# Zero matmuls during the first loads and two weight pieces ahead of the loop, in a windowed attention with a three-way max layer

## The chip, the cores and the metric

The kernel runs on one core of one Trainium2 chip. The core has a matrix engine (PE, TensorE), a vector engine (DVE), a scalar engine (ACT), a general engine (POOL, GpSimd) and a queue processor (SP, SyncE) that issues most transfers; sixteen DMA engines carry them. The metric is device time in microseconds of one execution; the median of some executions is compared.

## The reference

Eight batches of eight heads attend over 512 local and 32 global tokens of width 64. A local query sees the 32 global keys and the local keys at most 32 positions away; a global query sees all keys. The output of each token (8 heads by 64 = 512 numbers) goes through a layer with three weight matrices, an elementwise maximum, and an output matrix:

```python
k_all = np.concatenate([k_g, k_l], axis=2)
s_g = scale * np.matmul(q_g, k_all.transpose(0, 1, 3, 2))
out_g = np.matmul(sm(s_g), v_all)
mask = np.abs(pos[:, None] - pos[None, :]) <= window
s_ll = np.where(mask, s_ll, -1000000000.0)
a_l = sm(np.concatenate([s_lg, s_ll], axis=-1))
out_l = np.matmul(a_l, np.concatenate([v_g, v_l], axis=2))
...
h = np.maximum(np.maximum(x @ w1, x @ w2), x @ w3)
return (h @ w_out).astype(np.float32)
```

There are 4352 tokens (8 times 544). The maximum layer goes from 512 to 768 and back to 512. The weights arrive as 64-bit floats.

## The kernel before

**Attention.** Work is cut into 128 tiles `sl`: pair of heads `p = sl // 4`, and a quarter `t` of 128 queries. A tile passes these steps, each with an engine's line: `load_q` (L250) brings the queries, `scores` multiplies them with the window's keys on PE (L335 for the first 28 tiles, which are kept in f32) into a bank `S`, DVE adds the mask and scales and keeps the row extreme (L342), ACT takes the exponential and its sum (L344), DVE takes the reciprocal (L347, L348) and one of DVE, ACT and POOL multiplies (L121, L123, L125). `trans` turns the result on PE into a bank `T` (L362, L363), a copy takes it out as `pt`, and `pv` multiplies it with the values on PE (L401) into a bank `O`, copied to `xr`. `split_x` (L424, L425) makes a high and a low part of `xr`, the tile `xs`, which feeds the maximum layer. The first sixteen tiles go through the two halves of the queries in the order `SEQ`, with half key blocks from `load_half` (L216); their softmax lies in a constant tile `early`.

**Weights.** There are 24 pieces of 128 by 512 numbers: 18 of the three matrices and 6 of the output matrix. `load_weight` (L165) brings the 64-bit piece, 512 KB, into `raw`. `convert` makes two f32 parts of it on the chip, in three steps: ACT takes the absolute value of the high words (L175) and DVE does two scalar passes (L176, L177); DVE joins sign and low bits in two passes (L180, L181); a cast (L115 or L113) and a subtraction (L103, on DVE or POOL) give the high and the low part in `w`. `weight_step` (L192) advances every piece under way by one step, starts one piece, and calls `load_weight` once. From piece 6 on, a load waits until the absolute value of the piece five before it has been taken.

**Maximum layer.** `moe_local(b)` is a generator of PE matmuls for batch `b`: `layer1` (L441) and `layer2` (L463), with accumulation in three banks `pm`. `fill(n)` takes `n` of its matmuls into the program. Batch 0 is done in halves of 256 tokens; its first half starts to be emitted behind iteration 7.

**Order.** The prologue (L548 to L566) issues the first loads and the scores of tiles 0 to 2. The loop (L567) runs over the 128 tiles; iteration `i` transposes tile `i+1`, computes scores of tile `i+3`, does `pv` of tile `i`, fills PE with layer matmuls in four places, and ends with `weight_step` as often as the list `WS` says for `i` (27 calls in all). A planner turns this into one fixed order for each engine; it may take an instruction ahead of others of its engine, so `layer1` matmuls appear in the trace before the place where the program has them. Where an elementwise step may go to more than one engine, `least` chooses by running sums of estimated cost. All loads but the mask stand in SP's queue, in program order; SP waits there until a buffer is free.

Of the kernel before, what the change touches and what calls it, by code (L numbers as in the profile page):

```python
# [9 lines left out]
F32 = mybir.dt.float32  # L10
# [16 lines left out]
HIMAX = float(np.array(0x47EFFFFF, np.int32).view(np.float32))  # L27


UNITS = [0, 1, 2, 16, 3, 4, 5, 6, 7, 8, 9, 10, 16, 11, 12, 13, 14, 15]  # L30
WIN = [(0, 192), (96, 224), (256, 224), (384, 192)]

VROWS = []
for _o, _w in WIN:
    VROWS.append(UNITS[_o // 32:_o // 32 + 4])
    VROWS.append(UNITS[_o // 32 + 4:(_o + _w) // 32])

# [17 lines left out]
def body(ctx, tc, kin, qin, vin, min_, win, out):  # L55
    nc = tc.nc
    act, dve, pool, pe = nc.scalar, nc.vector, nc.gpsimd, nc.tensor

    const = ctx.enter_context(tc.tile_pool(name="const", bufs=1))
# [3 lines left out]
    pm = ctx.enter_context(tc.tile_pool(name="pm", bufs=3, space=PSUM))  # L63
# [68 lines left out]
    mask = const.tile([128, 2, 224], F32, name="mask")  # L132
    zero = small.tile([128, 1], F32, name="zero", bufs=1)
    dve.memset(zero, 0.0)
    prob = [const.tile([128, 2, 256], F32R, name=f"prob{i}") for i in range(2)]
    probg = [const.tile([128, 3, 128], F32R, name=f"probg{i}") for i in range(2)]
    qgz = const.tile([128, 2, 160], F32R, name="qgz")
# [22 lines left out]
    def load_weight():  # L160
        n = loaded[0]
        if n < 24:
            loaded[0] += 1
            raw[n] = const.tile([128, 512], mybir.dt.int64, name=f"raw{n}", tag=f"w{n}")
            d = nc.sync.dma_start(out=raw[n], in_=win[n])  # L165
            if n >= 6:
                tc.add_manual_dep(d.ins, marks[n - 5], SYNC, reason="pace")

    def convert(n):
        r = raw[n].bitcast(I32).rearrange("p (n t) -> p n t", t=2)  # L170
        if n < 18:
            c = spare[n // 2 % 2 if n < 15 else 1][:, n % 2]
        else:
            c = moe.tile([128, 512], I32, name="wct", tag="o", bufs=2)
        marks[n] = act.activation(out=f32(c), in_=f32(r)[:, :, 1], func=AF.Abs).ins.name  # L175
        dve.tensor_scalar(out=f32(c), in0=f32(c), scalar1=2.0 ** -15, scalar2=HIMAX, op0=ALU.max, op1=ALU.min)  # L176
        dve.tensor_scalar(out=c, in0=c, scalar1=0x07FFFFFF, scalar2=3, op0=ALU.bitwise_and, op1=ALU.logical_shift_left)  # L177
        spend("a", 520)
        yield
        dve.scalar_tensor_tensor(out=c, in0=r[:, :, 1], scalar=-0x40000000, in1=c, op0=ALU.bitwise_and, op1=ALU.bitwise_or)  # L180
        dve.scalar_tensor_tensor(out=c, in0=r[:, :, 0], scalar=29, in1=c, op0=ALU.logical_shift_right, op1=ALU.bitwise_or)  # L181
        spend("dx", 1900)
        yield
        wt[n] = const.tile([128, 1024], F32R, name=f"w{n}", tag=f"w{n}")
        copy(weight(n, 0), f32(c))
        sub(weight(n, 1), f32(c), f32(weight(n, 0)))
        yield
# [4 lines left out]
    def weight_step():  # L192
        for c in list(live):
            next(c[0])
            c[1] += 1
            if c[1] == 3:
                live.remove(c)
        n = next(todo, None)
        if n is not None:
            c = convert(n)  # L200
            next(c)
            live.append([c, 1])
        load_weight()
# [5 lines left out]
    SEQ = [4 * p + t for h in range(2) for p in range(NP) for t in (2 * h, 2 * h + 1)] + list(range(16, NS))  # L209
    kraw, kst, qraw, qs, vraw, vs, xr, sc, pg, pts = [{} for _ in range(10)]  # L210

    def load_half(i):
        h, p = divmod(i, NP)
        c0 = 256 * h
        t = att.tile([128, 320], F32, name="kh", tag="kst") if i % 3 < 2 else att.tile([128, 320], F32, name="kh", tag="kraw", bufs=1)
        nc.sync.dma_start(out=t, in_=kin[p, :, c0:c0 + 320])  # L216
        khalf[p] = (t, c0)
# [22 lines left out]
        sub(t[64:128, 0], r[0:64, 0:KW], f32(t)[0:64, 0])  # L240
        sub(t[0:64, 1], r[64:128, 0:KW], f32(t)[64:128, 1])

    def load_q(s):
        if s < NS:
            if s in NATK:
                e = s < EARLY and SEQ.index(s) % 2
                qraw[s] = att.tile([128, 256], F32, name="qn", tag="qraw" if e else "qs")
            else:
                qraw[s] = att.tile([128, 256], F32, name="qraw")
            nc.sync.dma_start(out=qraw[s], in_=qin[s])  # L250

    def split_q(s):
        if s < NS and s not in NATK:
            r = qraw.pop(s)
            t = qs[s] = att.tile([128, 2, 256], F32R, name="qs")
            copy(t[:, 0], r)
            sub(t[:, 1], r, f32(t)[:, 0])

    def load_v(s, spot=0):
        if s < NS:  # L260
            if spot % 5 < 3:
                vraw[s] = att.tile([128, 4, D], F32, name="vraw", bufs=3)
            else:
                vraw[s] = att.tile([128, 4, D], F32, name="vn", tag="vs")
            nc.sync.dma_start(out=vraw[s], in_=vin[s].rearrange("p (x d) -> p x d", d=D))
# [257 lines left out]

    mm = [None]

    WS = [1, 1, 1, 1, 1, 1, 2, 1, 1, 1, 2, 1, 1, 1, 2, 1, 1, 1, 1, 1, 1, 1, 1, 1]

    def fill(n):
        if mm[0]:
# [5 lines left out]
    def tile_at(i):  # L535
        return SEQ[i] if i < NS else NS

    def next_scores(last):
        while ahead[0] <= last:
            i = ahead[0]  # L540
            scores(tile_at(i))
            split_q(tile_at(i + 1))
            load_q(tile_at(i + 4 if i < 12 else i + 3))
            if i < 16 and i % 2 and i // 2 + 3 < 8:
                load_half(i // 2 + 3)
            ahead[0] += 1

    load_half(0)  # L548
    load_q(SEQ[0])
    act.dma_start(out=mask, in_=min_)  # L550
    load_q(SEQ[1])
    load_half(1)
    load_v(SEQ[0], 0)
    load_q(SEQ[2])
    load_q(SEQ[3])
    load_v(SEQ[1], 1)
    load_weight()
    load_half(2)
    load_weight()
    next_scores(1)  # L560
    load_v(SEQ[2], 2)
    load_weight()
    next_scores(2)
    load_v(SEQ[3], 3)
    load_weight()
# [1 line left out]
    for i, sl in enumerate(SEQ):  # L567
# [41 lines left out]
        else:  # L609
            load_v(tile_at(i + 4))  # L610
        for _ in range(WS[i] if i < len(WS) else 0):
            weight_step()
# [18 lines left out]
def _pack(q_l, k_l, v_l, q_g, k_g, v_g):  # L631
    kt = [k_l[:, :, 32 * u:32 * u + 32] for u in range(16)] + [k_g]
    k = np.concatenate([kt[u] for u in UNITS], axis=2).transpose(0, 1, 3, 2)
    k = np.ascontiguousarray(k).reshape(B, NP, 128, KW)
# [19 lines left out]
    for t, (o, w) in ((1, WIN[1]), (2, WIN[2])):  # L654
        for c, u in enumerate(UNITS[o // 32:(o + w) // 32]):
            for i in range(32):
# [30 lines left out]
```

## Time and profile before

Three runs gave 829.75, 829.39 and 828.55 us.

| | us |
|---|---|
| median of the three runs | 829.39 |
| the profiled execution | 831.31 |
| its span (first to last instruction) | 829.5 |
| PE busy in the span | 803.7 |
| DVE busy | 616.8 |
| ACT busy | 508.5 |
| POOL busy | 459.2 |

A profile line of the timeline gives start, duration, engine, line, operation, output and input, and in brackets the idle time before it with what ended it. A view by windows gives for each stretch the busy time of each engine with the number of instructions, then the granted clock of PE (1.00 is full), the busy share of the DMA engines, and GB/s. Matmul records overlap, since matmuls are pipelined, so a busy PE is not always PE at its peak. In the page's view of slices each digit is the busy share of 20.7 us in tenths.

The page's chain of work that ended last gives PE 86% of the span, with `layer1` 48% and `layer2` 17%.

### The profile page before, as it was taken

The numbers are of one execution on the slowest core, as the hardware profiler recorded it, in microseconds if no ns is written. First come the engines' busy times: TensorE is split into PE (matmuls) and PEld (weight loads), VectorE is DVE, ScalarE is ACT, GpSimd is POOL, SyncE is SP. The second block draws the span as 40 slices with busy tenths as digits, with TensorE's granted clock in tenths as the row PEclk, the third lists the DMA queues.
The fourth block names the chain that finished last, engine by engine and source line by source line (L and its number), as shares of the span: only waits on it lengthen the run. The fifth ranks groups of instructions, "written<-read, shape, count | busy, mean of one in ns | idle before, by whom it ended". The sixth has DMA issues, their size and how long they took to land.

```text
span 829.5 us, 16594 instructions
## 1 busy us (share of the span) xinstructions
PE 803.7 (97%) x4772; PEld 685.8 (83%) x4772; DVE 616.8 (74%) x2192; ACT 508.5 (61%) x1415; POOL 459.2 (55%) x624
## 2 busy tenths in 40 slices
PE   7788999999999999999999999999999999999996
PEld 5577888888888888888888888888888888888895
DVE  6999897878888888888897888888887887421121
ACT  5987786657666766667676667666676766311110
POOL 4223345756677676756676676866786665311110
PEclk9989999999999999999999999999999999999999
DMA  9856554433334433343335333443325332100101
GB/s 309 304 185 212 167 152 148 139 127 115 109 115 136 121 92 112 99 151 102 104 109 166 116 98 92 133 138 110 93 88 166 115 93 74 61 1 1 38 14 26
DMA packets 97467, 98.16 MB, mean 118 GB/s; under 512 B 19296, under 2 KB 85856, under 8 KB 97376
## 3 DMA queue, kind: packets, MB, share of 16 engines
q1 hardware_dynamic: 97232, 96.87, 37.5%
q8 instruction: 38, 0.62, 0.3%
q14 instruction: 53, 0.43, 0.2%
q10 hardware_dynamic: 144, 0.23, 0.1%
HBM read 60.39 MB, written 8.91 MB: 84 GB/s over the span
## 4 chain that ended last, share of the span: by engine, by line
PE 86%; DMA 5%; issue 3%; DVE 2%; SPq 1%; ACT 1%; POOL 1%; POOLq 0%; DVEq 0%; ACTq 0%
PE pm L441 48%; PE pm L463 17%; PE O L409 7%; PE S L339 5%; PE T L362 2%; DMA prob<-s 2%; DMA raw<-w_in 2%; PE T L363 2%; PE S L289 2%; PE S L335 1%; DMA vraw<-v_in 1%; PE S L381 1%; PE O L401 1%; POOL w L103 1%; DMA qn<-q_in 1%
## 5 line engine op out<-in xcount | busy, mean ns | idle before, releaser
L441 PE MATMUL pm<-xs,w 128*128 128x512 f32 (+1 forms) x2160 | 488.9, 367 | 1.3 <-ACT m L115 0.9
L441 PEld LDWEIGHTS pm<-xs,w 128*128 128x128 f32 x2160 | 355.9, 191 | 52.7 <-issue 4.2
L463 PE MATMUL pm<-w,h 128*128 128x512 f32 x612 | 156.4, 396 | 0.0
L103 POOL TENSOR_TENSOR h<-m,h 128x512 fp32r<-128x512 f32 (+1 forms) x59 | 70.6, 1197 | 109.8 <-ACT h L115 109.2
L463 PEld LDWEIGHTS pm<-w,h 128*128 128x128 f32 x612 | 109.4, 188 | 19.1 <-issue 0.2
L450 DVE TENSOR_TENSOR m<-pm,m 128x512 f32<-128x512 f32 (+1 forms) x120 | 72.8, 607 | 63.1 <-PE pm L441 62.3
L344 ACT ACTIVATE s<-s,nm 128x192 f32<-128x192 f32 (+1 forms) x224 | 103.3, 462 | 22.3 <-DVE nm L342 17.6
L103 POOL TENSOR_TENSOR qs<-qraw,qs 128x256 fp32r<-128x256 f32 x100 | 76.5, 765 | 69.1 <-issue 33.2
L125 POOL TENSOR_SCALAR s<-s,z 128x224 f32<-128x224 f32 (+1 forms) x194 | 84.9, 446 | 36.5 <-ACT lox L115 18.9
L342 DVE CUSTOM_DVE_ANT_0 s<-S,mask 128x192 f32<-128x192 f32 (+1 forms) x224 | 74.8, 370 | 16.3 <-PE S L339 7.7
L103 POOL TENSOR_TENSOR vs<-vraw,vs 128x256 fp32r<-128x256 f32 x102 | 75.0, 736 | 13.3 <-ACT vs L115 6.5
L103 DVE TENSOR_TENSOR pt<-T,pt 128x512 fp32r<-128x512 f32 x102 | 70.4, 690 | 15.2 <-ACT pt L115 13.8
L409 PEld LDWEIGHTS O<-pt,vs 128*128 128x128 f32 x408 | 65.9, 188 | 10.4 <-issue 2.4
L409 PE MATMUL O<-pt,vs 128*128 128x320 f32 (+1 forms) x408 | 73.1, 300 | 1.4 <-DVE pt L103 1.4
L115 ACT CAST pt<-T 128x512 fp32r<-128x512 f32 x102 | 60.3, 592 | 16.6 <-PE T L363 14.0
L339 PEld LDWEIGHTS S<-kst,qs 128*128 128x128 f32 x400 | 59.6, 190 | 8.7
L417 DVE TENSOR_TENSOR xr<-O,lox 64x160 f32<-64x160 f32 x204 | 64.3, 315 | 2.9
L103 POOL TENSOR_TENSOR kst<-kraw,kst 64x576 fp32r<-64x576 f32 x44 | 63.9, 1453 | 4.3 <-PE S L335 1.0
L115 ACT CAST h<-m 128x512 fp32r<-128x512 f32 (+1 forms) x59 | 33.2, 562 | 52.8 <-DVE m L450 52.5
L115 ACT CAST qs<-qraw 128x256 fp32r<-128x256 f32 x93 | 38.0, 409 | 44.0 <-PE S L339 31.1
L339 PE MATMUL S<-kst,qs 128*128 128x192 f32 (+1 forms) x400 | 59.5, 270 | 0.0
L347 DVE TENSOR_SCALAR z<-z 128x1 f32<-128x1 f32 x256 | 37.2, 147 | 27.3 <-ACT s L344 18.7
(123 smaller groups left out, 1183.0 us busy)
## 6 DMA issues: line engine op xcount, KB each, us to landing
vraw<-v_in SPq DMA_DIRECT2D x122, 128.0 KB, 2.3
qraw<-q_in SPq DMA_DIRECT2D x100, 128.0 KB, 2.1
prob<-s SPq DMA_DIRECT2D x56, 224.0 KB, 2.5
raw<-w_in SPq DMA_DIRECT2D x24, 512.0 KB, 4.9
prob<-s SPq DMA_DIRECT2D x56, 192.0 KB, 2.3
out_dram<-o SPq DMA_DIRECT2D x32, 256.0 KB, 2.6
kraw<-k_in SPq DMA_DIRECT2D x25, 320.0 KB, 3.1
qn<-q_in SPq DMA_DIRECT2D x29, 128.0 KB, 3.7
```

What stands on the lines that cost most here:

```text
L103: (dve if least(c) == "d" else pool).tensor_tensor(out=out, in0=a, in1=b, op=ALU.subtract)
L115: act.copy(out=out, in_=a)
L125: pool.tensor_scalar(out=out, in0=a, scalar1=col, scalar2=1.0, op0=ALU.mult, op1=ALU.mult)
L339: pe.matmul(ph[j][:, 0:n], lhsT=qs[sl][:, a, 128 * j:128 * j + 128], rhs=kst[p][:, j, c0:c0 + n], start=(a == 0), stop=(a == 1))
L342: dve.tensor_tensor_reduce(out=s[:, j, 0:n], in0=ph[j][:, 0:n], in1=mask[:, (1, 0, 1, 0)[t], 32 * (t == 0):32 * (t == 0) + n], scale=-0.12 ...
L344: act.activation(out=s[:, j, 0:n], in_=s[:, j, 0:n], func=AF.Exp, bias=nm[:, j:j + 1], scale=-1.0, accum_out=z[:, j:j + 1])
L347: dve.tensor_scalar(out=z[:, j:j + 1], in0=z[:, j:j + 1], scalar1=1e-9, scalar2=None, op0=ALU.add)
L409: pe.matmul(o[:, j, 0:320].rearrange("p (a q) -> p a q", a=2)[:, :, 0:n], lhsT=vs[sl][:, 2 * j + c].rearrange("p a d -> p (a d)"), rhs=pt[ ...
L417: dve.tensor_tensor(out=xr[p][64 * j:64 * j + 64, t], in0=o[0:64, j, 0:160], in1=lo[:, j], op=ALU.add)
L441: pe.matmul(ps[:, 0:n], lhsT=weight(3 * f + i, w)[:, 128 * k:128 * k + 128], rhs=xs[k][:, a, c0:c0 + n], start=(q == 0), stop=(q == 11))
L450: dve.tensor_tensor(out=m[:, 0:n], in0=ps[:, 0:n], in1=m[:, 0:n], op=ALU.max)
L463: pe.matmul(banks[t], lhsT=hh[f][:, a, 128 * t:128 * t + 128], rhs=weight(18 + f, w), start=((f, a, w) == (0, 0, 0)), stop=((f, w) == (5, 1)))
```

## The change

It defines a zeroed 128 by 128 tile `nil` and multiplies it six times with itself on PE, into a `pm` bank that nothing reads, as the first work of PE. It reorders the first loads: the queries of tiles 0 and 1 go through ACT's queue, the mask through SP's; the first weight piece is the third load on SP, the second is the seventh. It calls `weight_step` twice ahead of the loop, once behind the scores of tile 0 and once behind those of tile 1, each of which starts a piece and loads one. In `WS`, the 2 at iterations 6 and 10 become 1, so that there are 27 steps as before.

```diff
+BLANK = 6
...
+    nil = const.tile([128, 128], F32, name="nil")
+    dve.memset(nil, 0.0)
...
-    def load_q(s):
+    def load_q(s, eng=nc.sync):
...
-            nc.sync.dma_start(out=qraw[s], in_=qin[s])
+            eng.dma_start(out=qraw[s], in_=qin[s])
...
-    WS = [1, 1, 1, 1, 1, 1, 2, 1, 1, 1, 2, 1, 1, 1, 2, 1, 1, 1, 1, 1, 1, 1, 1, 1]
+    WS = [1, 1, 1, 1, 1, 1, 1, 1, 1, 1, 1, 1, 1, 1, 2, 1, 1, 1, 1, 1, 1, 1, 1, 1]
...
+    blank = pm.tile([128, 512], F32, name="pm")
+    for _ in range(BLANK):
+        pe.matmul(blank[:, 0:128], lhsT=nil, rhs=nil, start=True, stop=True)
     load_half(0)
-    load_q(SEQ[0])
-    act.dma_start(out=mask, in_=min_)
-    load_q(SEQ[1])
+    load_q(SEQ[0], act)
+    nc.sync.dma_start(out=mask, in_=min_)
+    load_q(SEQ[1], act)
+    load_weight()
     load_half(1)
+    load_q(SEQ[2])
     load_v(SEQ[0], 0)
-    load_q(SEQ[2])
+    load_weight()
     load_q(SEQ[3])
     load_v(SEQ[1], 1)
-    load_weight()
     load_half(2)
-    load_weight()
+    next_scores(0)
+    weight_step()
     next_scores(1)
     load_v(SEQ[2], 2)
-    load_weight()
+    weight_step()
     next_scores(2)
     load_v(SEQ[3], 3)
     load_weight()
```

## The prediction, made before the changed kernel ran

> **What bounds the kernel now.** The page comes first: engine shares and slices.
>
> ```profile
> PE 803.7 (97%) x4772; PEld 685.8 (83%) x4772; DVE 616.8 (74%) x2192; ACT 508.5 (61%) x1415; POOL 459.2 (55%) x624
> PE   7788999999999999999999999999999999999996
> DVE  6999897878888888888897888888887887421121
> ```
>
> TensorE is busy 803.7 of 829.5 us, so at most 25.8 us of idle time and whatever runs at a low clock can go. The low digits are the first four slices of 20.7 us, and there DVE is the fuller engine. The change works in that stretch, so the view by windows of the first 170 us is read next. Its columns are busy us and instructions of PE, its weight loads, DVE, ACT and POOL, then granted clock, DMA share, GB/s.
>
> ```profile
> 0.00:4.40 4.40, 0.02 (x1) 0.05 (x1) 0.54 (x2) 1.28 (x1) 2.17 (x15) 1.00 0.57 156
> 4.40:10.00 5.60, 5.26 (x19) 4.69 (x20) 3.04 (x22) 2.77 (x10) 0.00 (x0) 1.00 0.97 317
> 10.00:20.00 10.00, 8.86 (x67) 6.34 (x68) 9.61 (x40) 7.80 (x26) 5.98 (x9) 1.00 1.02 368
> 20.00:30.00 10.00, 8.38 (x62) 5.73 (x60) 9.65 (x37) 8.15 (x22) 2.79 (x3) 1.00 1.02 365
> 30.00:38.00 8.00, 6.67 (x48) 4.95 (x46) 8.00 (x28) 7.61 (x22) 1.30 (x1) 1.00 0.82 259
> 38.00:43.40 5.40, 1.68 (x12) 1.09 (x12) 5.40 (x16) 4.42 (x13) 1.62 (x1) 0.90 0.44 157
> 43.40:49.10 5.70, 5.67 (x24) 5.22 (x24) 5.70 (x21) 5.41 (x16) 1.28 (x1) 0.50 0.11 28
> 49.10:60.00 10.90, 10.90 (x96) 10.05 (x94) 9.10 (x30) 8.17 (x23) 3.24 (x3) 1.00 0.85 284
> 60.00:70.00 10.00, 9.60 (x70) 7.51 (x66) 10.00 (x36) 9.07 (x26) 3.59 (x4) 1.00 0.74 244
> 80.00:90.00 10.00, 8.25 (x50) 6.73 (x52) 8.69 (x29) 6.14 (x20) 3.36 (x4) 0.83 0.49 151
> 150.00:170.00 20.00, 20.00 (x128) 16.92 (x128) 16.41 (x63) 12.69 (x35) 16.26 (x21) 0.96 0.47 150
> ```
>
> Three things are to be seen. From 10 to 49 us DVE has no room (9.61 of 10, 9.65 of 10, then full), while PE waits for what DVE makes. There is one hole: at 38.0 to 43.4 us PE is busy 1.68 of 5.40 us, 3.72 idle, and behind it PE works 5.70 us at a granted clock of 0.50, another 2.85 us lost. By 150 us PE is full and remains the bound. So time saved early stays saved only as far as PE gets its work sooner; after 150 us nothing here changes.
>
> **What the start looks like.** The timeline of the first microseconds, and later rows of the same operations:
>
> ```profile
> 0.73 0.39 ACTq L550 DMA_DIRECT2D mask<-m_in  x1
> 0.74 0.41 SPq L216 DMA_DIRECT2D kh<-k_in  x1
> 0.97 0.48 DVE L155 MEMSET T<- 128x512 f32 x1
> 1.16 1.28 ACT L344 ACT_TABLE_LOAD   x1 [1.16 <-PEq L679]
> 4.38 4.94 PE L335 MATMUL S<-kh,qn 128*128 128x192 f32 x16 [4.38 <-DMA qn<-q_in]
> 4.38 3.11 PE L335 MATMUL S<-kh,qn 128*128 128x192 f32 x8 [4.38 <-DMA qn<-q_in]
> 6.04 0.36 DVE L342 CUSTOM_DVE_ANT_0 early<-S,mask 128x192 f32<-128x192 f32 x1 [4.58 <-PE S L335]
> 6.44 0.46 ACT L344 ACTIVATE early<-early,nm 128x192 f32<-128x192 f32 x1 [4.00 <-DVE nm L342]
> 7.53 0.39 DVE L342 CUSTOM_DVE_ANT_0 early<-S,mask 128x224 f32<-128x224 f32 x1 [0.85 <-PE S L335]
> 9.26 0.67 ACT L175 ACTIVATE spare<-raw 128x512 f32<-128x512 f32 x1 [0.25 <-DMA raw<-w_in]
> 16.45 0.92 PE L335 MATMUL S<-kh,qn 128*128 128x192 f32 x4
> 19.13 0.51 PE L441 MATMUL pm<-xs,w 128*128 128x256 f32 x2
> ```
>
> DVE does no more than its memsets until 6.04 us, then waits another 0.85 us, both times for score matmuls (L335). A tile is four of these instructions, sixteen are four tiles. By the same view over 4 to 7 us the first eight take 3.11 us, 0.39 each; the four at 16.45 take 0.92, 0.23 each, the last one's tail included. So the first ones run slow although the clock column says 1.00 there; the durations decide. The sixteen stand in one piece: after 4.38 PE isn't waiting for loads, its own speed sets when DVE starts.
>
> **The change, part by part.** *Blanks.* Six f32 matmuls of 128 columns are twelve instructions. At 0.39 us for 192 to 224 columns (mean 208), one of 128 is 0.39×128/208 = 0.24 and the twelve take 2.9 us. They need the `nil` memset on DVE; by the T memset (512 columns, 0.48) it is 0.12 to 0.2 us, in time DVE is idle. So they run from about 1.2 to 4.1 us. Queued behind them on PE is the first score, and DVE waits for that; the cover is the wait for the first loads, and without it they would cost their 2.9 us.
>
> *First loads.* `q` of tiles 0 and 1 goes to ACT's queue, the mask to SP's second place. Landing times per tile in the first 13 us, for `mask`, then `kh`, then `raw`:
>
> ```profile
> DMA to landing us min/median/max: 3.1/3.1/3.1
> DMA to landing us min/median/max: 3.3/4.7/5.4
> DMA to landing us min/median/max: 4.7/5.4/6.4
> ```
>
> `q` in the mask's place lands about 0.73+3.1 = 3.8, and `kh` 0.74+3.3 = 4.0. The first score starts near 4.0 instead of 4.38 (4.1 if the blanks are the later). The mask, issued at 1.2, lands near 4.4, before DVE needs it. On ACT two issues of 0.39 push the table load (1.28) to about 2.9 us; its first user stands at 6.44, so it is covered by 2 us even if that comes 1.5 earlier.
>
> [...]
>
> Bounds for DVE's first work, from those rows: if the scores remain slow, 0.38 us earlier (the start); if all are fast, tile 0 takes 0.92 instead of the 1.66 from 4.38 to 6.04, so it is 0.38+0.74 = 1.12 earlier, and the 0.85 us wait for tile 1 goes too: 2.0. I take **1.3 us**, the middle rounded up, since twelve instructions of work go ahead of tile 1.
>
> *Weights forward.* One piece passes five stages on DVE. Their rows for the first piece:
>
> ```profile
> 11.05 0.41 DVE L176 TENSOR_SCALAR spare<-spare 128x512 f32<-128x512 f32 x1
> 11.52 0.41 DVE L177 TENSOR_SCALAR spare<-spare 128x512 int32<-128x512 int32 x1
> 13.12 0.68 DVE L180 SCALAR_TENSOR_TENSOR spare<-raw,spare 128x512 int32<-128x512 int32 x1
> 15.15 0.69 DVE L181 SCALAR_TENSOR_TENSOR spare<-raw,spare 128x512 int32<-128x512 int32 x1
> 17.77 0.42 DVE L113 CAST w<-spare 128x512 fp32r<-128x512 f32 x1
> 18.28 1.27 POOL L103 TENSOR_TENSOR w<-spare,w 128x512 fp32r<-128x512 f32 x1 [0.41 <-DVE w L113]
> 18.33 1.77 DVE L180 SCALAR_TENSOR_TENSOR spare<-raw,spare 128x512 int32<-128x512 int32 x1
> 31.82 0.70 ACT L175 ACTIVATE spare<-raw 128x512 f32<-128x512 f32 x1
> 32.84 0.67 ACT L175 ACTIVATE spare<-raw 128x512 f32<-128x512 f32 x1
> ```
>
> Four stages are always DVE's: 0.41+0.41+0.68+0.69 = 2.2 us; the cast or the subtraction adds up to 0.7. (Beside POOL's subtraction one such stage took 1.77 instead of 0.68; which engine gets it is set by the running load sums and can fall either way.) Two pieces, 4.4 us, go ahead of the loop; the list `WS` gives one back at iteration 6 and one at 10, so the total stays 27 steps and DVE's work sum is unchanged. The gain is only that the first stages fall where DVE idled. The first piece, third on SP, is issued near 1.7 and lands, at the least time of 4.7, near 6.4 instead of 9.2, so its Abs on ACT ends near 7.1. By then DVE has done tiles 0 and 1 and has waited again; the lead stays the 1.3 us above and I count nothing on top. The Abs is a new early wait: behind it on ACT stand the exponentials (6.44 now), and if it is placed in front of tile 0's, they wait until 6.4+0.7, which would cost their lead of 1.3 us.
>
> *The double steps.* The two Abs at 31.82 and 32.84 are iteration 6's double step: one piece's 2.2 us of DVE time stands there in front of scores, just ahead of the hole. Rows inside the hole:
>
> ```profile
> 40.63 1.02 PE L335 MATMUL S<-kh,qn 128*128 128x224 f32 x4 [1.36 <-DVE nm L342]
> 43.43 0.47 PE L362 MATMUL T<-one,early 128*128 128x128 f32 x1 [1.77 <-ACT early L123]
> ```
>
> PE waits for a score's DVE pass and then for a normalization on ACT, both fed by the full DVE queue. What the hole gives back lies between 0 (it only moves) and 3.72+2.85 = 6.6 us (it closes and the clock stays up). I take **2.2**, one piece's DVE time, because DVE is full there and that is what leaves its queue.
>
> *SP.* Every load is behind the earlier pieces. `q` of tile 3, `v` of tile 1 and `kh` 2 stood ahead of any piece or behind one, and stand now behind two. At 365 GB/s, the rate in 20 to 30 us where the DMA share is 1.02, 524 KB is 1.4 us. In the loop one piece more is ahead of each load: 1.4 us. The scores of 16.45 and their like show no DMA wait now, so I count 0; the other end is the rival below. `pm` lends the blanks one of three buffers until about 4 us; its first user stands at 19.13, so no wait follows.
>
> **Sum.** 1.3 + 2.2 = 3.5 us. The profiled run took 831.31 us for a span of 829.5, thus 827.8 in its terms; it lies 1.9 above the median of the three runs, 829.39, so on the median **825.9 us**.
>
> **Rivals.** (B) *The hole and its clock drop vanish.* For it: the drop at 43.4 follows directly on 3.7 idle us, so a smaller hole may take it away whole. Against: 80 to 90 us shows another (0.83) with DVE at 8.69, so drops may just move. 2.0+6.6 = 8.6 us: 820.8.
>
> (C) *The lead is handed back.* By iteration 10 the same pieces are done, and DVE is full again at 60 to 70 us; the clock may stay low in the start and the hole may only shift. It leaves between 0.4 and 1.3 us: about 828.7. [...]
>
> (D) *Loads become the bound, slower.* The place is the score of tile 3: its `q` is behind two pieces, 2.8 us later, while the DMA share is 0.97 to 1.02. Then PE, whose 0.38 earlier start is gone, waits for loads instead of DVE's results: 2.8-0.4 = +2.4, 831.8. It decides once waits of scores on DMA after 6 us exceed the 1.3 us won. Against it: DVE has the first piece to work on meanwhile.
>
> **How the numbers follow.** Forecast A (823.5 to 827.7) 0.45; B 0.13; C 0.24; D 0.18. About 0.2%, 1.7 us, is what a measurement of this kernel can tell from no change: faster by more is A and B, 0.58; within is C, 0.24; slower is D, 0.18. The range runs from B's end, 820.8, to D's, 831.8; outside lie the worse half of D and a little of B.
>
> **What would show it.** Right: the first DVE score pass near 4.7 us; four score matmuls in about 0.92 us by tile 1; the first Abs near 6.5; PE's idle time in 38 to 44 us under 2 us with a clock above 0.5 behind it. Wrong: scores still at 0.39 us each when tile 1 runs (blanks useless); PE waiting on `qn` after 6 us (D); the same hole with the same clock drop elsewhere before 60 us (C); or a total of PE idle time in the first 150 us that has not fallen by 2 us.

## The result: 6 us slower, and the profile after

The changed kernel takes **835.35 us** (median of 14 runs, 832.06 to 837.59), the kernel before 829.34 (14 runs on the same chips, 826.7 to 832.27). The ratio is 1.0068, with a 95% interval of 1.0055 to 1.0081. The forecast was 825.9 us, with a range up to 831.8: so the sign was wrong, and the time lies above the range.

A profile is one execution, and executions of one kernel differ in their granted clock: from 80 to 90 us it is 0.83 in the first profile of before and 1.00 in the second. The first profile of before (span 829.5 us) was among its longer runs, the first of after (830.2) is the shortest of its 14. So a second profile of the kernel before, with a span of 825.8 us, the shortest of nine new runs, stands beside it from here on. These new runs have a median of 829.12 against 829.53 for other runs of the same kernel, ratio 0.9998 (0.9984 to 1.0011).

The page of after: busy time and count of each engine.

```profile
PE 804.1 (97%) x4784; PEld 684.9 (82%) x4784; DVE 616.3 (74%) x2196; ACT 508.5 (61%) x1415; POOL 457.8 (55%) x621
```

DVE's busy total is what it was (616.8 before), so the change moved its work and did not add to it. The view by windows of after:

```profile
10.00:20.00 10.00, 7.38 (x53) 5.22 (x52) 8.83 (x37) 7.16 (x23) 5.12 (x6) 0.93 1.05 383
20.00:30.00 10.00, 8.70 (x57) 6.00 (x55) 9.79 (x32) 8.26 (x24) 2.30 (x2) 0.90 0.85 281
30.00:38.00 8.00, 5.75 (x33) 4.33 (x32) 8.00 (x29) 6.90 (x20) 2.02 (x2) 0.85 0.59 190
38.00:43.40 5.40, 5.21 (x35) 3.69 (x34) 4.39 (x19) 4.12 (x13) 0.93 (x1) 0.91 0.63 186
43.40:49.10 5.70, 4.42 (x32) 3.48 (x31) 4.68 (x19) 4.96 (x18) 0.36 (x1) 1.00 0.86 257
...
100.00:120.00 20.00, 18.96 (x167) 15.68 (x166) 19.70 (x62) 15.23 (x46) 8.69 (x8) 1.00 0.47 137
120.00:150.00 30.00, 26.22 (x231) 23.47 (x230) 21.19 (x97) 20.14 (x63) 14.94 (x22) 1.00 0.48 139
...
0.00:60.00 60.00, 48.75 (x313) 37.70 (x313) 50.93 (x192) 45.04 (x128) 17.18 (x28) 0.94 0.78 259
60.00:170.00 110.00, 102.18 (x814) 87.80 (x813) 96.88 (x359) 79.66 (x235) 52.61 (x62) 1.00 0.56 171
```

and of before, second profile:

```profile
30.00:38.00 8.00, 6.84 (x50) 5.12 (x48) 8.00 (x30) 7.59 (x23) 1.30 (x1) 1.00 0.82 267
38.00:43.40 5.40, 2.23 (x12) 1.34 (x12) 5.40 (x14) 4.42 (x12) 1.62 (x1) 0.79 0.42 154
43.40:49.10 5.70, 5.49 (x27) 5.07 (x28) 5.70 (x23) 5.42 (x16) 1.27 (x1) 0.60 0.07 17
...
100.00:120.00 20.00, 20.00 (x179) 17.10 (x177) 18.41 (x68) 16.87 (x52) 9.92 (x8) 1.00 0.51 151
120.00:150.00 30.00, 27.19 (x258) 24.52 (x258) 23.72 (x93) 18.59 (x57) 16.23 (x24) 1.00 0.53 162
...
0.00:60.00 60.00, 48.63 (x320) 38.95 (x320) 51.45 (x189) 46.18 (x128) 18.35 (x33) 0.94 0.79 268
60.00:170.00 110.00, 104.43 (x816) 88.93 (x816) 96.80 (x363) 80.57 (x239) 53.61 (x64) 1.00 0.55 169
```

The hole at 38 to 43 us is gone, as forecast: PE is busy 5.21 of 5.40 us, and the clock behind it is 1.00. But PE has lost as much around it: 7.38 of 10 us in 10 to 20 (8.86 in the first profile of before), 5.75 of 8 in 30 to 38, with granted clocks of 0.93 to 0.85.

Busy time says little of progress in these first 60 us, since a slow matmul counts as busy (the first eight scores are 3.11 us of work in before and 2.12 in after). The counts say more. Both kernels have the same matmuls but for the twelve blanks (4772 and 4784 instructions). By 60 us before has done 320, after 313−12 = 301; by 170 us it is 320+816 = 1136 against 313+814−12 = 1115. But 19 behind and then 21 behind are not the same loss, because matmuls differ in size. The view by lines says which ones are missing. By 80 us all that after lacks are twelve `layer1` matmuls of 256 columns; by 170 us it lacks fourteen `layer2` matmuls of 512 columns and a few small ones. Before's second profile, then after, first to 80 us, then to 170:

```profile
L441 PE MATMUL pm<-xs,w 128*128 128x256 f32 x181 | 32.3, 311 | 1.3 <-ACT m L115 0.9 <-DVE xs L103 0.4
L444 PE MATMUL pm<-xs,w 128*128 128x256 f32 x169 | 29.1, 309 | 0.5 <-DVE xs L104 0.3 <-ACT xs L116 0.2
...
L463 PE MATMUL pm<-w,h 128*128 128x512 f32 x61 | 16.0, 398 | 0.0
L466 PE MATMUL pm<-w,h 128*128 128x512 f32 x47 | 12.4, 398 | 0.0
```

By the page of after the 612 `layer2` matmuls are busy 156.3 us, 0.255 us each. At that rate, an estimate, fourteen are 3.6 us; twelve of half the columns are about 1.5 us. The two spans differ by 4.4 us. So **about a third of the loss is there by 80 us, and most of the rest comes between 100 and 150 us**, where the granted clock is 1.00 in both profiles and PE is busy 18.96+26.22 = 45.2 us in after and 20.00+27.19 = 47.2 in before.

**The start worked.** The timeline of after:

```profile
1.08 2.93 PE L553 MATMUL pm<-nil 128*128 128x128 f32 x12 [1.08 <-DVE nil L137]
3.88 2.12 PE L338 MATMUL S<-kh,qn 128*128 128x192 f32 x8
5.29 0.36 DVE L345 CUSTOM_DVE_ANT_0 early<-S,mask 128x192 f32<-128x192 f32 x1 [3.67 <-PE S L338]
6.05 0.39 DVE L345 CUSTOM_DVE_ANT_0 early<-S,mask 128x224 f32<-128x224 f32 x1
6.08 0.66 ACT L178 ACTIVATE spare<-raw 128x512 f32<-128x512 f32 x1 [3.17 <-DMA raw<-w_in]
6.78 0.43 DVE L179 TENSOR_SCALAR spare<-spare 128x512 f32<-128x512 f32 x1
7.10 0.89 PE L338 MATMUL S<-kh,qn 128*128 128x192 f32 x4 [1.09 <-DMA qn<-q_in]
7.24 0.43 DVE L180 TENSOR_SCALAR spare<-spare 128x512 int32<-128x512 int32 x1
7.70 0.69 DVE L183 SCALAR_TENSOR_TENSOR spare<-raw,spare 128x512 int32<-128x512 int32 x1
9.37 0.67 DVE L184 SCALAR_TENSOR_TENSOR spare<-raw,spare 128x512 int32<-128x512 int32 x1
10.34 0.41 DVE L179 TENSOR_SCALAR spare<-spare 128x512 f32<-128x512 f32 x1
10.66 0.35 DVE L345 CUSTOM_DVE_ANT_0 early<-S,mask 128x192 f32<-128x192 f32 x1
```

The blanks take the 2.9 us forecast, eight scores take 2.12 us in place of 3.11, and DVE starts tile 1 at 6.05 without a wait, 1.5 us before the old kernel (7.53). Then the lead is spent: five passes of weight pieces stand on DVE between 6.78 and 10.66, and tile 2's first score pass, which in before's second profile starts at 8.90, starts at 10.66, though its scores are done by 7.99. The lead of 1.5 us is a lag of 1.8 within 5 us.

### The profile page after: what moved, and what is told of

Its sections match the earlier page's. It is cut to its first block, busy times and chain, and to the rows that moved or that the text cites. A ratio compares the mean times of both kernels' runs of the same rounds, so it can differ in the third digit from the quotient of the medians.

```text
span 830.2 us, 16623 instructions
## 1 busy us (share of the span) xinstructions
PE 804.1 (97%) x4784; PEld 684.9 (82%) x4784; DVE 616.3 (74%) x2196; ACT 508.5 (61%) x1415; POOL 457.8 (55%) x621
## 4 chain that ended last, share of the span: by engine, by line
PE 85%; DVE 6%; DMA 3%; ACT 2%; issue 2%; POOL 1%; SPq 0%; POOLq 0%; DVEq 0%; ACTq 0%
PE pm L444 47%; PE pm L466 17%; PE O L412 7%; PE S L342 5%; PE T L365 2%; PE T L366 2%; PE S L292 2%; PE S L338 1%; PE O L404 1%; DMA vraw<-v_in 1%; DVE spare L183 1%; PE S L384 1%; DMA qn<-q_in 1%; DVE spare L179 1%; ACT s L347 0%
## 5 line engine op out<-in xcount | busy, mean ns | idle before, releaser
L466 PE MATMUL pm<-w,h 128*128 128x512 f32 x612 | 156.3, 396 | 0.0
L126 POOL TENSOR_SCALAR s<-s,z 128x192 f32<-128x192 f32 (+1 forms) x197 | 86.2, 445 | 37.7 <-ACT lox L116 18.9
L412 PEld LDWEIGHTS O<-pt,vs 128*128 128x128 f32 x408 | 65.9, 188 | 10.8 <-issue 2.1
L420 DVE TENSOR_TENSOR xr<-O,lox 64x160 f32<-64x160 f32 x204 | 64.3, 315 | 3.0
```

The source lines that it names most:

```text
L126: pool.tensor_scalar(out=out, in0=a, scalar1=col, scalar2=1.0, op0=ALU.mult, op1=ALU.mult)
L412: pe.matmul(o[:, j, 0:320].rearrange("p (a q) -> p a q", a=2)[:, :, 0:n], lhsT=vs[sl][:, 2 * j + c].rearrange("p a d -> p (a d)"), rhs=pt[ ...
L420: dve.tensor_tensor(out=xr[p][64 * j:64 * j + 64, t], in0=o[0:64, j, 0:160], in1=lo[:, j], op=ALU.add)
L466: pe.matmul(banks[t], lhsT=hh[f][:, a, 128 * t:128 * t + 128], rhs=weight(18 + f, w), start=((f, a, w) == (0, 0, 0)), stop=((f, w) == (5, 1)))
```

## The experiments

In what follows the first number is the kernel's median, the second that of the kernel before on the same chip, then their ratio and its 95% interval.

**1. The parts alone.** Four kernels: the six zero matmuls alone in the old kernel; the change without them; the new first loads alone; the two early steps with the new `WS` alone.

```diff
 e1: before, and
+    nil = const.tile([128, 128], F32, name="nil")
+    dve.memset(nil, 0.0)
+    for _ in range(6):
+        pe.matmul(blank[:, 0:128], lhsT=nil, rhs=nil, start=True, stop=True)
 e2: the change without these
 e3: before, and the first loads of the change (load_q on act, mask on SP,
     first load_weight third, second seventh)
 e4: before, and
+    next_scores(0)
+    weight_step()
     next_scores(1)
     load_v(SEQ[2], 2)
-    load_weight()
+    weight_step()
     and the list WS of the change
```

> Only the six zero matmuls and their memset are added; loads, steps and WS are as before. If the pieces ahead of the loop make the change slow (theory P), this lies at 828 to 829.5 us: the first scores are faster, DVE starts at most 1.1 us earlier. If the early rise of the clock shifts where it falls later (theory W), it lies near the changed kernel, 833 to 836. If only the order of the first loads is to blame (theory L), as under P.

> The changed kernel without the zero matmuls. Theory P: still slow, 834 to 837 us, the blanks giving back at most 1.5 us. Theory W: back at 829 to 831. Theory L: still slow, 834 to 837.

> Only the new order of the first loads (q of tiles 0 and 1 on ACT's queue, mask on SP, first piece third, second seventh); no step ahead, WS as before, no blanks. Theory P: within 1.7 us of before (829 to 831), since the pieces wait for their converting anyway. Theory L: 833 to 836, tiles 2 and 3 late by the pieces' 2.9 us. Theory W: 829 to 831.

> Only the two steps ahead of the loop and the changed WS; the first loads in the order of before, no blanks. Theory P: slow, 833 to 837 us, with PE's lag behind its own work over 1.5 us greater than before at 30 us. Theories W and L: 828 to 830.

| | this | before | ratio | interval |
|---|---|---|---|---|
| e1, six zero matmuls | 831.57 | 828.25 | 1.0033 | 1.0016 to 1.0050 |
| e2, change without them | 832.79 | 828.25 | 1.0052 | 1.0033 to 1.0072 |
| e3, new loads | 830.74 | 828.25 | 1.0026 | 1.0011 to 1.0040 |
| e4, two early steps | 833.07 | 828.25 | 1.0061 | 1.0040 to 1.0083 |

No part helps. The two steps alone make 4.8 of the 6 us, the others 2.5 and 3.3, and they don't add up. e2 also shows what the blanks do to the first scores, with the same loads. The timeline of e2:

```profile
3.94 3.11 PE L336 MATMUL S<-kh,qn 128*128 128x192 f32 x8 [3.94 <-DMA kh<-k_in]
...
11.22 1.70 PE L336 MATMUL S<-kh,qn 128*128 128x224 f32 x4
```

Without the blanks eight scores take 3.11 us and four at 11.22 still 1.70; with them 2.12 and, at 7.10, 0.89. So the scores run faster behind the zero matmuls, although the clock column says 1.00 from 0 to 10 us in both profiles. This settles what the bounds of the prediction left open, for this order of loads: the scores don't all stay slow. It is not so in every kernel: in e1, where PE idles 0.49 us behind the blanks and the scores start at 4.50, tile 0's first score pass stands at 6.16, 1.66 us behind that start, as in before (4.38 and 6.04). In after it is 1.41 (3.88 and 5.29). What makes e1 differ these traces don't show.

**2. Is it the clock?** Zero matmuls keep PE busy behind the value products of nine early tiles, in both kernels. They go into the unused half of the bank `O`.

```diff
+            if 0 < SEQ.index(sl) < 10:
+                for _ in range(4):
+                    pe.matmul(o[:, 1, 0:128], lhsT=nil, rhs=nil, start=True, stop=True)
```

> The kernel before once more, for a second profile beside the first one, whose own time of 831.31 us was the highest of its runs. Every theory: 827 to 831 us. If the clock drops set how far an execution is above 827 us, a profile of a shorter one has fewer of them than the first profile's three before 160 us, and PE's lag behind its own work at 50 us is smaller by the missing drop.

> Before, with four zero matmuls behind the value products of the tiles at places 1 to 9 of SEQ, into the half of the O bank that is not used there: PE has eight instructions of about 0.11 us more per tile, so that its clock stays up. Theory W (drops of the clock make the difference): 826 to 828.5 us, little better than before, with no drop in 10 to 50 us. Theory P (the pieces ahead make attention late): 827 to 831, the zero matmuls take PE time where it is idle.

> The changed kernel with the same zero matmuls. Theory W: within 1.5 us of the kernel before kept warm, 826 to 829. Theory P: 3.5 to 5 us above it, 831 to 834, since the values of tiles 4 to 9 come late whatever the clock.

> Before with one step ahead of the loop instead of two (behind the scores of tile 1) and the 2 of iteration 6 made 1; loads in the old order, no blanks. Theory P: half of the 4.8 us of both steps, 830 to 831.5. Theory W: no clear order, 828 to 833. If the double step at iteration 10 is what has to stay for the order to be good, 828 to 829.

Before with this: 827.72 against 829.53, ratio 0.9987 (0.9971 to 1.0004). After with it: 834.12 against 829.53, ratio 1.0062 (1.0040 to 1.0083). The windows of before with the extra matmuls:

```profile
38.00:43.40 5.40, 5.40 (x41) 4.19 (x41) 5.40 (x14) 3.84 (x11) 1.35 (x1) 1.00 0.64 225
43.40:49.10 5.70, 5.46 (x42) 4.88 (x41) 4.96 (x22) 5.24 (x15) 1.28 (x1) 1.00 0.25 61
```

The hole is filled (PE busy 5.40 of 5.40 us) and the clock is 1.00 through it, and that is worth 1.1 us by the ratio, 2.4 at the end of its interval, perhaps nothing (the extra matmuls can also shift the planner's order, see part 3). The prediction had put a price of up to 6.6 us on hole and drop. The changed kernel with the same filling has its clock at 1.00 from 20 to 49 us, but at 0.66 from 10 to 20, and is 6.4 us above it. With that drop it doesn't settle the question.

The mean granted clock of each execution, which stands in the record beside its time, does. Its median is 0.994 in the runs of before beside the parts above. It is 0.995 in e4 and 0.9955 in e2, and 0.997 and 0.996 in two variants of the changed kernel in part 3 (h2, h4). These four are 4.5 to 6.9 us slower than before at a clock that is no lower. **So most of the loss isn't the clock.** A share of it can be: after's own median is 0.991, and 0.003 of 829 us, an estimate of its price, is 2.5 us, out of 6.

The fourth kernel of this group (g1) takes one step ahead instead of two, with the old loads and no blanks:

```diff
-    WS = [1, 1, 1, 1, 1, 1, 2, 1, 1, 1, 2, ...]
+    WS = [1, 1, 1, 1, 1, 1, 1, 1, 1, 1, 2, ...]
     load_v(SEQ[2], 2)
-    load_weight()
+    weight_step()
```

It takes **837.51** against 829.53, 1.0085 (1.0060 to 1.0110): half the early work costs more than all of it. So "weight work ahead costs time by its amount" can't be the whole story, and something else must change with it. Its median clock, 0.994, is no lower than before's.

**3. The planner's order.** The same edit can also shift instructions that it does not touch, since the planner orders each engine anew. Five blanks leave the order of everything else in before as it was; with six, 101 lines of PE's order differ. Two kernels move the order with work that matters to nobody, and one has the change with five blanks.

```diff
 h1: before with BLANK = 5
 h2: the change, and
+    dve.memset(dud0, 0.0)           # 128x1
 h3: before, and
+    pool.memset(dud0, 0.0)          # 128x256
+    pool.memset(dud1, 0.0)          # 128x256
 h4: the change with BLANK = 5
```

> Before with five zero matmuls instead of six. With five the planner's order of all other instructions is word for word that of before; with six, 101 lines of PE's order differ from it. Theory O (the planner's new order costs, not the blanks): 827 to 829.5 us, at or below before, where six blanks took 831.6. Theory W (the blanks' own effect on PE's clock): 831 to 832, as with six.

> The changed kernel with one more DVE memset of 128x1 (about 0.06 us, while DVE is idle) at the start. The memset's own cost is under 0.1 us, but 92 lines of PE's order change. Theory O: the time moves by more than 1.5 us to either side, outside 834 to 836.5. Theory P (the amount of DVE work put ahead of attention): 834 to 836.5 as the changed kernel.

> Before with two POOL memsets of 128x256 at the start, in time POOL is idle; 32 lines of PE's order and 12 of DVE's differ. Theory O: if before's order is a favourable one, 829.5 to 833 us. If the order of few lines doesn't matter, 827.5 to 829.5.

> The changed kernel with five zero matmuls instead of six: 0.25 to 0.5 us less PE work in the first 4 us, and 102 lines of PE's order differ. Theory O: outside 834 to 836.5 us. Theories P and W: inside it.

| | this | before | ratio | interval |
|---|---|---|---|---|
| h1, before, five blanks, same order | 829.08 | 828.19 | 1.0011 | 1.0002 to 1.0020 |
| h2, after, 92 PE lines reordered | 834.05 | 828.19 | 1.0078 | 1.0060 to 1.0096 |
| h3, before, 32 PE lines reordered | 827.04 | 828.19 | 0.9993 | 0.9976 to 1.0010 |
| h4, after, 102 PE lines reordered | 835.07 | 828.19 | 1.0081 | 1.0067 to 1.0096 |

Five blanks in the same order cost 0.9 us, six in another order 3.3. The mean granted clock goes with that: its median is 0.990 in e1, 0.994 in h1 and before, and 0.004 of 828 us, an estimate of its price, is 3.3 us. e1's only execution at 0.994 took 827.68 us, h1's only one at 0.990 took 831.07. So e1 has the lower clock, 0.989 to 0.991, in nine of ten executions; whether the sixth blank or the other order brings it isn't shown. The changed kernel stays at 834 to 835 under two other orders, and the old one stays at 827 under another. The 6 us are not one unlucky order.

**4. The choice of engine.** `least` chooses by running sums of cost, and an early `weight_step` spends early, so later choices fall another way. Of the 24 casts of weights (L115, L113) before gives 6 to DVE, after 10; of their subtractions (L103) 11 and 8. The view by groups of the first 80 us has the normalization of the early tiles, in before's second profile

```profile
L123 ACT ACTIVATE early<-early,z 128x224 f32<-128x224 f32 x10 | 4.7, 475 | 0.0
L123 ACT ACTIVATE early<-early,z 128x192 f32<-128x192 f32 x10 | 4.5, 450 | 0.6 <-DVE z L347 0.3 <-DVE z L348 0.3
```

and in after

```profile
L124 ACT ACTIVATE early<-early,z 128x192 f32<-128x192 f32 x13 | 5.9, 454 | 1.5 <-DVE z L351 1.4
L124 ACT ACTIVATE early<-early,z 128x224 f32<-128x224 f32 x12 | 5.8, 483 | 1.1 <-DVE z L350 1.1
```

Five of POOL's nine have gone to ACT: 25 of 32 instead of 20, and PE's transposes `T` wait for them (for ACT 3.6 us against 2.4 in 10 to 50 us, for POOL 1.9 against 0.8, by the view of waits). To test it, the list of choices of one kernel is recorded and given to another, so that only the choices, or only the rest, differ. With its own choices, e4 has those of after, e3 those of before.

```diff
-        es = min(costs, key=lambda es: max(load[e] for e in es) + costs[es])
+        e = next(chosen[caller])
+        es = next(x for x in costs if x[0] == e)
```

> The changed kernel, but each elementwise step goes to the engine that it had in before (a list of before's choices, by place and number, is replayed). Theory E (the choice of engines): 828 to 830.5 us. Theory P (the place of the steps): 833 to 836.

> Before, with the list of the changed kernel's choices replayed; loads, steps and WS as before, no blanks. Theory E: 833 to 836 us. Theory P: 827 to 830.

> One step ahead of the loop, as in the run with 837.5 us, with before's choices replayed. Theory E: 828 to 831 us. Theory P: 834 to 838.

| | this | before | ratio | interval |
|---|---|---|---|---|
| j1, after, before's choices | 833.60 | 828.10 | 1.0065 | 1.0041 to 1.0088 |
| j2, before, after's choices | 833.86 | 828.10 | 1.0064 | 1.0045 to 1.0083 |
| j3, one step ahead, before's choices | 827.73 | 828.10 | 0.9995 | 0.9980 to 1.0009 |

The choices alone are worth nearly as much as the whole change: they make the old kernel 5.8 us slower (j2), and giving g1 those of before takes it from a ratio of 1.0085 to 0.9995 (j3), which is 7.5 us. That explains why one step ahead cost more than two: its own choices were worse. With them held still, one step costs nothing that can be measured. But j1 refuses the simple end of the story: the changed kernel with before's choices is as slow as with its own.

**5. What else keeps the changed kernel slow.** With before's choices in all three: the two steps alone (k1), and the loads with the six blanks (k2, whose own choices are those of before). The third run is a candidate: j3 with the zero matmuls of part 2.

```diff
 k1: j3, and
+    next_scores(0)
+    weight_step()
     next_scores(1)
-    WS = [1, 1, 1, 1, 1, 1, 1, 1, 1, 1, 2, 1, ...]
+    WS = [1, 1, 1, 1, 1, 1, 1, 1, 1, 1, 1, 1, ...]
 k2: e1 and e3 together
 k3: j3, and the zero matmuls behind nine value products
```

> Edit: before with the two early steps and the new list WS alone (old first loads, no blanks), and before's choice of engine for each elementwise instruction. Theory P (what keeps the changed kernel slow under before's choices, 833.6 us, is the new loads and the six zero matmuls): with the choices put back the steps alone cost little, 828 to 830 us, ratio 0.999 to 1.002. Theory Q (it is the second early step itself, for which no choice made for before fits): 832 to 835 us, ratio 1.005 to 1.008, like the same steps with their own choices (833.07). Between 830 and 832: both have a share.

> Edit: before with the new first loads and the six zero matmuls, no early step and the old list WS; the engine choices come out as in before. Alone the loads cost 2.1 us and the six zero matmuls 2.8 us. Theory P (loads and zero matmuls keep the changed kernel slow under before's choices): 832 to 834 us, ratio 1.005 to 1.007. Theory Q (the second step does): no more than the larger of the two alone, 829.5 to 831 us, ratio 1.002 to 1.0035.

> Edit: one step ahead of the loop, old loads, before's engine choices (this measured 827.73 us), and four zero matmuls behind the value products of tiles 1 to 9 that keep the clock up. A candidate to beat both kernels. If the two small gains (0.4 us for the step with before's choices, 1.3 to 1.8 us for the zero matmuls in before) add: 826 to 827 us, ratio 0.997 to 0.999. If each only stands for a lucky order: 827.5 to 830 us, ratio 0.999 to 1.003.

| | this | before | ratio | interval |
|---|---|---|---|---|
| k1, two steps, before's choices | 834.86 | 829.24 | 1.0076 | 1.0055 to 1.0097 |
| k2, loads and six blanks | 832.64 | 829.24 | 1.0043 | 1.0026 to 1.0060 |
| k3, j3 kept busy | 827.58 | 829.24 | 0.9992 | 0.9976 to 1.0008 |

j3 and k1 have the same choices; they differ in the second step ahead, in where the list gives it back, and in the order that the planner then makes. **Their ratios are 0.9995 and 1.0076, and the two intervals are well apart.** Part of this goes with the clock: the medians are 0.996 in j3 and 0.990 in k1. At an equal clock, 0.994, one execution of each took 829.79 and 833.02 us, so some 3 us remain. Whether the delay brings the lower clock isn't shown. Loads and blanks have their own smaller price. k3 can't be told from the old kernel; no kernel here beats it measurably.

Two runs from above complete the picture. e4 has the two steps and the choices of after: ratio 1.0061. j2 has these choices and no step: 1.0064. **With the choices of after the two steps cost nothing measurable on top; with those of before they cost 5.6 us (k1).** Either change by itself reaches about the whole loss, and the two don't add.

Where the second step costs its time can be read in the timeline of DVE. j3, one step ahead:

```profile
13.03 0.69 DVE L140 COPY pt<-T 128x512 f32<-128x512 f32 x1
...
16.06 0.68 DVE L140 COPY pt<-T 128x512 f32<-128x512 f32 x1
16.66 0.34 DVE L369 CUSTOM_DVE_ANT_0 early<-S,mask 128x192 f32<-128x192 f32 x1
```

k1, two steps ahead:

```profile
11.66 0.68 DVE L207 SCALAR_TENSOR_TENSOR spare<-raw,spare 128x512 int32<-128x512 int32 x1
...
13.81 0.68 DVE L140 COPY pt<-T 128x512 f32<-128x512 f32 x1
...
15.56 0.80 DVE L207 SCALAR_TENSOR_TENSOR spare<-raw,spare 128x512 int32<-128x512 int32 x1
...
16.36 1.42 DVE L203 TENSOR_SCALAR spare<-spare 128x512 f32<-128x512 f32 x1
17.70 0.68 DVE L208 SCALAR_TENSOR_TENSOR spare<-raw,spare 128x512 int32<-128x512 int32 x1
18.30 0.59 DVE L204 TENSOR_SCALAR spare<-spare 128x512 int32<-128x512 int32 x1
18.81 0.67 DVE L140 COPY pt<-T 128x512 f32<-128x512 f32 x1
19.41 0.34 DVE L369 CUSTOM_DVE_ANT_0 early<-S,mask 128x192 f32<-128x192 f32 x1
```

Weight passes run from 11.66 to 13.8 where j3 takes out its first transposed tile. Four more, 3.5 us, stand between 15.56 and 18.81; one of them takes 1.42 us, where j3's takes 0.41 at 14.62. So the second such copy (`pt`) slips from 16.06 to 18.81. From there the score passes, and with them everything that feeds PE, are late. The starts of the first score pass of five tiles, from such rows:

| tile | before, second profile | j3, one step | k1, two steps | after |
|---|---|---|---|---|
| 4 | 14.78 | 16.66 | 19.41 | 16.41 |
| 9 | 33.84 | 36.95 | 40.87 | 37.74 |
| 10 | 40.06 | 40.06 | 44.57 | 41.02 |
| 14 | 59.24 | 58.91 | 61.34 | 59.28 |
| 15 | 64.03 | 62.78 | 67.36 | 64.71 |

One step ahead makes tile 9 3.1 us late, and the double step that then falls away at iteration 6 pays that back: tile 10 starts at 40.06 in both. The second step makes tile 9 another 3.9 us late and is repaid only behind tile 10: of the 4.5 us by which tile 10 is late, 2.1 are left at tile 14, and tile 15 is 3.3 us behind before. The changed kernel is 3.9 us late at tile 9 too, but only 1.0 at tile 10, not at all at tile 14, and 0.7 at tile 15: there the delay is nearly repaid. Nor do late tiles explain every slow kernel: in g1 the second score pass of tile 15 starts at 65.5, 1.2 us behind before's 64.3, and the span is 10.8 us longer.

The windows of PE, j3 first, then k1, then j2:

```profile
0.00:60.00 60.00, 46.56 (x321) 36.45 (x322) 51.45 (x193) 45.22 (x129) 20.05 (x33) 1.00 0.80 261
60.00:170.00 110.00, 103.99 (x818) 89.12 (x819) 95.66 (x360) 80.60 (x240) 54.15 (x64) 1.00 0.55 173
```

```profile
0.00:60.00 60.00, 44.04 (x266) 33.46 (x267) 48.13 (x182) 42.18 (x120) 19.44 (x32) 0.91 0.77 249
60.00:170.00 110.00, 104.05 (x841) 89.82 (x840) 95.68 (x356) 82.00 (x239) 53.43 (x60) 1.00 0.56 171
```

```profile
0.00:60.00 60.00, 48.34 (x312) 37.99 (x312) 50.57 (x186) 44.69 (x127) 17.07 (x28) 0.94 0.77 266
60.00:170.00 110.00, 99.99 (x795) 84.89 (x796) 96.15 (x359) 79.57 (x236) 50.99 (x60) 1.00 0.53 162
```

By 60 us k1 has done 266 matmuls against 321 in j3 and wins only 23 of the 55 back by 170. j2 loses in another place: it is only 8 small ones behind before by 60 us, and 21 more by 170. Two different ways lead to 29 behind 1136, and to spans of 830.8 and 831.7.

The second way is that of the choices. Between 60 and 170 us ten profiles have a granted clock of 1.00. In the five with before's choices PE is busy 103.6 to 104.5 us (104.43 in before), in the five with those of after 100.0 to 102.4 (102.18 in after, 102.27 in e4, 99.99 in j2). So the changed kernel, too, loses 2.25 us there, more than the 1.5 us that it is behind at 80.

## Why the prediction was wrong

**Right.** Blanks (2.9 us), first absolute value (6.08; forecast 6.5), fast scores by tile 1, tile 1's wait gone: a lead of 1.5 us there, where 1.3 was forecast. The first score pass came at 5.29 (forecast 4.7, old 6.04), so for tile 0 the lead is about half of it. That the scores would run faster behind zero matmuls was the author's estimate, which no run had shown; the runs showed 2.12 us for the first eight in after, 3.11 in e2, and in e1 a first score pass as far behind its scores as in before. The hole at 38 us fell from 3.7 idle us to 0.2. But the sign that the prediction itself set is against it: in the first 150 us PE's busy time did not rise, 130.96 us in after and 131.37 in the first profile of before, and 2.93 of after's are blanks. The wait of rival D appears once, 1.09 us on tile 2's queries, below the price at which D was to decide. That the loads alone (e3) cost 2.5 us, about D's 2.4, doesn't bear D out: by 60 us e3's PE has done 319 matmuls against 320 in before's second profile, and it falls back later (60 to 170 us: 807 at a clock of 0.98, against 816 at 1.00).

**The step that failed** is in *Weights forward*: "the total stays 27 steps and DVE's work sum is unchanged. The gain is only that the first stages fall where DVE idled", with nothing counted on the other side. The sum is indeed unchanged. But two things were put at nothing.

The first is the place in DVE's order. The prediction had itself read DVE as full from 10 us on, and of the 4.4 us of early work only the first passes had idle time to fall into. The rest stands in the fixed order of DVE ahead of the attention tiles that feed PE: tile 4 is 1.6 us late in after, tile 9 3.9 late. Work moved ahead on a full engine delays what stands behind it until the place where the list leaves it out. With before's choices held, two such steps cost 5.6 us (k1) and one costs nothing (j3). In after, where most of the delay is repaid by tile 14, PE is about 1.5 us behind at 80 us.

The second stood in parentheses: which engine gets a cast or a subtraction "can fall either way". It was left without a price. Measured by itself it is 5.8 us in the old kernel (j2), and 7.5 between g1 and j3, and the larger part of after's loss lies where j2's does, behind 60 us. In the changed kernel, though, it isn't what can be put right: with before's choices (j1) it is as slow, and then it is behind early, by 320−(288−12) = 44 matmuls at 60 us.

**The second term, 2.2 us for the hole, was the wrong kind of gain.** The hole was the place where the first piece's delay would be repaid, not time over and above: j3 shows it, late by 3.1 us at tile 9 and level at tile 10, ratio 0.9995. The second step has its place of repayment at iteration 10, and k1 shows it repaid in part. Rival C said this ("the hole may only shift") and stopped at a gain of 0.4 us; rival D, the only slower case, looked at the loads. What was missing is C with a negative end, and a rival in which the redrawn choices cost time.

**The size put on the hole** (up to 6.6 us with its clock drop) was also too high: filled with zero matmuls in the old kernel it gave 1.1 us by the ratio, not surely more than nothing.

What stays open: why the new loads alone cost 2.5 us though DVE starts sooner with them (first score pass at 5.60 in e2, 6.04 in before); why the prices of steps, choices, loads and blanks, each measured, don't add in the changed kernel; how much of each goes with a lower clock; and which instruction on the wrong engine makes j2 slow from 60 us on.

## What to carry to other kernels

When work is moved ahead on an engine with a fixed order, find the engine's idle time at the new place and charge everything beyond it to what stands behind; the place where it was taken out is the repayment, not a second gain. In a kernel whose planner chooses engines by running sums, a moved step redraws choices far behind it: hold the choices still in one experiment before explaining anything. And try half of the change: here it was slower than the whole, which showed that a second cause was at work. When two kernels are compared by counts of matmuls, look at their sizes: here lags of 19 and 21 matmuls stood for quite different times.

## What was not expected of the hardware and the program

Eight scores took 2.12 us behind zero matmuls (after), 3.11 without them (e2). Zero matmuls in the hole, with a clock of 1.00 through it where before's second profile has 0.79 and then 0.60, gave about 1 us of 829, with an interval that includes nothing. And a choice of engines that hardly touches the sums of work moves this kernel by 6 to 7.5 us (j2 against before, g1 against j3), more than any edit to its start won. Last, the times of the old kernel go with their mean granted clock: its 21 runs beside e1 have a median of 831.1 us at 0.991 and below, 827.8 at 0.994 and above.
